# Attention plan with new numbers, and a GpSimd operation per head that waits for VectorE's low part of v

## The chip, the core and the metric

One core of a Trainium2 chip runs the whole program. The metric is the device time of one execution in microseconds (us), taken as the median of several runs. Engines go by the profile's names: PE is TensorE (PEld its weight loads), DVE is VectorE, ACT is ScalarE, POOL is GpSimd, SP is SyncE, which issues the DMAs.

## The reference, cut to what matters

```python
def _attn_ref(q, k, v):                       # 2 x 8 heads, 1152 x 64
    q_pool = q.reshape(B, H, S // 2, 2, D).mean(axis=3)      # 576 queries
    scores = scale * np.matmul(q_pool, k.transpose(0, 1, 3, 2))
    scores = scores - np.max(scores, axis=-1, keepdims=True)
    attn = np.exp(scores)
    attn = attn / (np.sum(attn, axis=-1, keepdims=True) + 1e-09)
    return np.matmul(attn, v)
def reference(...):
    x = attention, heads side by side         # 1152 x 512
    x = _moe_ref(x, ...)                      # 4 experts: relu(x @ w1) @ w2, weighted
    return _moe2_ref(x, ...)                  # ((x@w1) * (x@w2)) @ w3 @ w_out
```

All of it is wanted in fp32 accuracy, so operands are split in a high and a low 16-bit part and multiplied in several passes.

## The kernel before

Attention goes by pairs of heads: pair i (0 to 7) holds heads s = 0 and s = 1; the first four pairs belong to batch 0, the others to batch 1. The work of a head is planned with these names, which are also the tiles' names in the rows:

- `plan_k`, `plan_q` (for the next pair): PE transposes k (kt, in two groups) and the pooled q (qt); ACT copies the high parts (kab, qh, and QZ, a bf16 copy of q); DVE subtracts to the low parts (kl line 281, ql line 332). A small cast of QZ stands on POOL (line 336), and POOL also pools q (QP, lines 246 and 249).
- `plan_max` (for the next pair): for nine blocks of queries PE makes rough scores mp (three matmuls of 384 columns, line 399) and DVE reduces them to maxima mx (two reductions, line 402); end of a head: mf (lines 416 to 419), a transpose mr on PE, a cast mh on ACT, and two small DMAs (lines 439, 440) that put the maxima into row 0 of Q2.
- `plan_v`: DVE takes v's row maxima (vm, line 468), PE spreads them (vp, line 472), and three short DVE operations (lines 456 to 460) make the scale vs. `v_hi` is the high part of v on ACT (line 521). `v_lo` is its low part on DVE: one SCALAR_TENSOR_TENSOR of 128 x 576 elements, line 525, two inputs in SBUF, one per head.
- `plan_scores`: per head nine chunks c: PE makes s (four matmuls, line 546), ACT takes the exponential pf (line 556), POOL subtracts the high half to get the low part pl (TENSOR_TENSOR 128 x 576, line 567, both inputs in SBUF). With two PSUM buffers for s, chunk c + 2 waits for pf of chunk c.
- `plan_av`: 135 small matmuls av per head (lines 589, 591), spread over the time of the next head; the first 27 need all nine chunks of pf and pl. `out_of` (DVE, lines 595 to 606) divides and stores; for batch 1 it has one operation more (XT, line 606).

PE's scratch tiles in PSUM are `work(0)` and `work(1)`, with one buffer each: kt, qt, mp, mr and vp take turns in them, and each waits until the one before has been read.

Nothing orders this at run time but the queues. Every step is put on an agenda with a time in chunks (`at(t, f)`), a head being 9 and a pair 18 of them; the agenda is sorted by that time and the steps are recorded in that order, so each engine's queue is the agenda's order. The numbers at the head of the file (lines 11 to 84) are those times. Semaphores for data and buffers are added by the framework. After the agenda, the experts and the last layers are recorded in a fixed order.

```python
def v_lo(i, s):
    src = rv[i][:, s, :].rearrange("p (c d) -> p c d", d=D)
    nc.vector.scalar_tensor_tensor(
        out=vt[s][:, :, 0:64], in0=src, scalar=vs[i][:, s : s + 1], in1=vt[s][:, :, 64:128],
...
nc.gpsimd.tensor_tensor(out=o, in0=f, in1=h, op=ALU.subtract)      # pl
```

Of the kernel before, what the change touches and what calls it, by code (L numbers as in the profile page):

```python
# [9 lines left out]

TURN = 0.985
TURNS = (1.141, 1.53, 3.03)
TURN0 = (0.042, 0.45, 0.848)
KH = 0.39
KL_ = 0.22
QH_ = 1.05
QL_ = 0.218
M0 = 0.122
M1 = 0.01
M2 = 0.49  # L20
LO_DVE = ((), ())
LASTD = ((3,), (1, 6))
LOL = 2.043
EX = 0.728
EX2 = 0.85
LO = 3.649
LOV = 1.281
AV0 = 1.49
AVN = 7.43
AVW = ((1.06, 0.102, 0.51, 0.636, 1.56, 0.106, 0.4, 2.814), (0.861, 0.24, 1.106, 3.116, 1.062, 0.51, 0.69, 1.54))  # L30
VH = 0.57
VL = 1.96
VL0 = -1.66
VR = 4.22
VE = 0.962
V1 = (5.587, 1.434)
VL1 = 7.087
QZ0 = 0.149
QZ1 = 0.0
VLZ = 2.729  # L40
K0 = 1.197
Q0 = 0.51
L0 = (5.7, 5.655)
LV2 = 16.124
PQ = 1.38
PQS = -2.45
SH = -6.018
XR = 138.482
CX = 129.207
CXT = (0, 0.419, 0.7, 1.3, 1.3)  # L50
LK1 = -10
LQ1 = -10
LV1 = -9
V0 = -8
V0E = -5.866
WARM = 39
WARM_K = 10
WARM_N = 5
WARM_E = 45
WARM_T = 8  # L60
VH0 = 1.5
FIRST = (0.71, 1.14, 2.08, 3.212)
NEAR = 0.0
LATER = 0
KT = (3.05, 4.25)
QT = 4.94
MX0 = (7.048, 8.195, 9.5, 11.42, 13.11)
SPOS = ((0, 1.3, 1.8, 2.8, 4.254, 4.9, 5.614, 6.855, 8.026), (-0.075, 0.604, 1.815, 2.935, 4.1, 4.548, 5.55, 6.8, 7.711))
AVS = 0.02
AVP = 1.7  # L70
MXF = (7.173, 8.254, 9.678, 11.809, 13.01)
MX1 = (14.249, 16.073, 17.228, 18.72)
ME = 0.17
SW = 130.75
W1 = 133.8
WT = ((124.735, 129.6, 130.611, 132.455, 138.5, 133.3, 133.5, 135.131, 135.8), (4.4, 8.95))
WN = (1, 4, 5, 3, 0)
WN2 = (1, 4, 4, 3, 0)
WS = 6
XA = 0.2  # L80
XS = 0.35
XC = (0.88, 1.1)
UA = 135.2
US = 2.59
DT = (140.727, 144.042)
OUT = 0.65
XB = 147.376
DS = 1.912
TICKS = ((), (), (), (0, 1), (), (2,), (0, 4, 13), (2, 9), (), (0, 2, 10), (2, 8, 9), (14,), (0, 10), (2,), (2, 6, 14), (2, 4, 7), (0, 1))
FT = ((7,), (5,), (3,), (4,), (7,), (3,), (), (4,))  # L90
GT = ((0, 2), (2,), (0, 1, 2), (0, 2), (0, 1), (0, 1), (), (0,))
# [13 lines left out]
ALU = mybir.AluOpType  # L105
# [12 lines left out]
def tile_kernel(ctx: ExitStack, tc: tile.TileContext, q, k, v, dp, w1, w2, mw1, mw2, mw3, mwo, out):  # L118
    nc = tc.nc
# [78 lines left out]
    QP = k_p.tile([P, NB + 1, 2, D], F32, name="QP")  # L198
# [39 lines left out]
    def at(t, f, *args):  # L238
        agenda.append((t, len(agenda), f, args))


    def pool_q(i, n):
        eng = nc.gpsimd if i else nc.vector
        if n < 2:
            x = rq[i][:, n]
            eng.tensor_tensor(out=QP[:, :NB, n, :], in0=x[:, :, 0, :], in1=x[:, :, 1, :], op=ALU.add)
        else:
            x = rt[i]
            eng.tensor_tensor(out=QP[:TL, NB], in0=x[:, :, 0, :], in1=x[:, :, 1, :], op=ALU.add)

    def work(g, name):

# [5 lines left out]
    def plan_k(i, t):  # L258
# [7 lines left out]
        for g in range(2):  # L266
# [54 lines left out]
    def plan_q(i, t, tv):  # L321
# [55 lines left out]
    def plan_max(i, s, times):  # L377
# [141 lines left out]
    def v_hi(i, s):  # L519
        src = rv[i][:, s, :].rearrange("p (c d) -> p c d", d=D)  # L520
        nc.scalar.activation(out=vt[s][:, :, 64:128], in_=src, func=AF.Copy, scale=vs[i][:, s : s + 1])

    def v_lo(i, s):
        src = rv[i][:, s, :].rearrange("p (c d) -> p c d", d=D)
        nc.vector.scalar_tensor_tensor(  # L525
            out=vt[s][:, :, 0:64], in0=src, scalar=vs[i][:, s : s + 1], in1=vt[s][:, :, 64:128],
            op0=ALU.mult, op1=ALU.subtract,
        )
# [3 lines left out]
    def plan_scores(i, s, t):  # L532
        for c in range(NC):
            st = {}

            def pe(c=c, st=st):
                if c == 0:
                    if i + s:
                        pft[i, s] = ph_p.tile([P, NC, T], F32, tag="pf", name=f"pf{i}_{s}")
                    pht[i, s] = pft[i, s].bitcast(BF16).rearrange("p c (t w) -> p c t w", w=2)[:, :, :, 1]  # L540
                    plt[i, s] = ph_p.tile([P, NC, T], F16, tag="pl", name=f"pl{i}_{s}")
                ps = st["s"] = ps_s.tile([P, 2, 512], F32, tag="s", name=f"s{i}_{s}_{c}")
                cs = slice(c * P, (c + 1) * P)
                for a, b, first in ((K2, Q2, True), (K1, Q1, False)):
                    for n in range(2):
                        mm(  # L546
                            ps[:, n, :HALF], a[s][:, cs], b[s][:, n * HALF : (n + 1) * HALF],
                            start=first, stop=not first,
                        )

            two = lambda ap: ap.rearrange("p (n t) -> p n t", n=2)

            on_dve = c in (LO_DVE[s] if i < NPAIR - 1 else LASTD[s])

            def whole(c=c, st=st):
                nc.scalar.activation(out=two(pft[i, s][:, c, :]), in_=st["s"][:, :, :HALF], func=AF.Exp, scale=SCORE)  # L556

            def again(c=c, st=st):
                x = st["s"][:, :, :HALF]
                nc.scalar.activation(out=x, in_=x, func=AF.Exp, scale=SCORE)  # L560

            def lo(c=c, st=st, on_dve=on_dve):
                o, f, h = plt[i, s][:, c, :], pft[i, s][:, c, :], pht[i, s][:, c, :]
                if on_dve:
                    nc.vector.tensor_tensor(out=two(o), in0=st["s"][:, :, :HALF], in1=two(h), op=ALU.subtract)
                else:
                    nc.gpsimd.tensor_tensor(out=o, in0=f, in1=h, op=ALU.subtract)  # L567

            u = t + (SPOS[s][c] if i else c)
            at(u, pe)  # L570
            at(u + EX, whole)
            if on_dve:
                at(u + EX2, again)
            at(u + (LOV if on_dve else LO if i < NPAIR - 1 else LOL), lo)

    def plan_av(i, s, t, span):
# [287 lines left out]
    with tc.manual_schedule():  # L864
# [489 lines left out]
```

## Time and profile before

| what | us |
|---|---|
| median of 3 runs (801.87 to 801.97) | 801.97 |
| the profiled execution | 798.73 |
| its span, first to last instruction | 796.9 |
| PE busy in the span | 777.3 |
| DVE busy | 592.3 |
| ACT busy | 398.9 |
| POOL busy | 293.9 |

The clock granted to PE was full in the whole span. Attention runs from about 18 us to about 238 us of the span; the experts and the last layers follow. In a row of the trace the first number is the start in us from the start of the span; a matmul's duration contains its pipeline's latency, so the pace of PE is read from start to start. A number in brackets is the engine's idle time just before, and what ended it.

### The profile page before, as it was taken

Reading aid. Unit: us, or ns where it says so; the run is one execution under the profiler, and the core shown is the slowest. Engines: PE = TensorE matmul, PEld = TensorE weight load, DVE = VectorE, ACT = ScalarE, POOL = GpSimd, SP = SyncE. Lnnn points to the kernel's source line nnn. Section 1 sums busy time; section 2 is a strip of 40 time slices with the busy share of each in tenths; the row PEclk is TensorE's granted clock in tenths of the full one; section 3 lists DMA queues with packets and bytes.
Section 4 is the critical chain, followed back from the end, with each engine's and each line's share of the span. In section 5 each row is a group of like instructions: output and inputs, shape, how many; then the busy total and the mean of one; then the engine's idle time right before and its main releaser. Section 6 shows DMA issues by size and latency. Waiting matters only on the chain.

```text
span 796.9 us, 15559 instructions
## 1 busy us (share of the span) xinstructions
PE 777.3 (98%) x6301; PEld 493.3 (62%) x6301; DVE 592.3 (74%) x1048; ACT 398.9 (50%) x722; POOL 293.9 (37%) x277
## 2 busy tenths in 40 slices
PE   8799999999999999999999999999999999999998
PEld 6588778877775555555555455554544445655787
DVE  6989898888956577789789999979978866872000
ACT  3666666656746432355334667544545544553111
POOL 5888988898640000011001223203331314343100
PEclk9999999999999999999999999999999999999999
DMA  7876676665311311223223242212367832200111
GB/s 176 211 169 146 167 176 146 154 148 125 91 29 53 106 53 54 80 82 116 93 68 93 79 131 79 83 53 79 107 132 151 176 109 80 80 1 1 27 40 53
DMA packets 86656, 79.68 MB, mean 100 GB/s; under 512 B 50425, under 2 KB 69113, under 8 KB 86585
## 3 DMA queue, kind: packets, MB, share of 16 engines
q1 hardware_dynamic: 86584, 78.70, 38.3%
q8 instruction: 49, 0.80, 0.4%
q14 instruction: 23, 0.18, 0.1%
HBM read 51.92 MB, written 2.36 MB: 68 GB/s over the span
## 4 chain that ended last, share of the span: by engine, by line
PE 75%; DVE 19%; DMA 3%; ACT 1%; issue 1%; SPq 0%; ACTq 0%
PE dn L760 19%; PE up L720 18%; PE gt L1292 12%; PE o L1308 6%; DVE mx L402 6%; PE wf L1261 5%; PE s L546 4%; PE mp L399 3%; PE av L591 3%; DVE vt L525 3%; DMA rw<-in_moe_w 2%; PE av L589 1%; DVE kl L281 1%; DVE vm L468 1%; DVE w L691 1%
## 5 line engine op out<-in xcount | busy, mean ns | idle before, releaser
L760 PE MATMUL dn<-w,h 128*128 128x512 f16 x840 | 184.1, 379 | 0.4 <-DVE h L731 0.4
L567 POOL TENSOR_TENSOR pl<-pf 128x576 f16<-128x576 f32 x141 | 164.4, 1196 | 10.9 <-ACT pf L556 10.3
L720 PEld LDWEIGHTS <-w 128*128 128x128 f16 x1152 | 111.6, 98 | 76.3 <-DVE w L691 1.0
L760 PEld LDWEIGHTS <-h 128*128 128x128 f16 x840 | 81.4, 98 | 96.7 <-issue 1.0
L556 ACT ACTIVATE pf<-s 128x576 f32<-128x576 f32 x144 | 93.0, 650 | 48.6 <-PE s L546 47.4
L402 DVE TENSOR_REDUCE mx<-mp 128x1 f32<-128x768 f32 (+1 forms) x144 | 101.9, 751 | 19.2 <-PE mp L399 16.7
L720 PE MATMUL up<-xB,w 128*128 128x320 f16 x768 | 109.9, 299 | 0.5 <-DVE xB L809 0.5
L859 POOL TENSOR_TENSOR wo<-wo,cv_a 128x512 f32<-128x512 f32 x20 | 25.8, 1292 | 225.0 <-DVE wo L856 126.9
L726 ACT ACTIVATE up<-up 128x320 f32<-128x320 f32 (+1 forms) x96 | 45.9, 478 | 115.3 <-PE up L720 103.6
L546 PE MATMUL s<-Q,K 128*128 128x288 bf16 (+1 forms) x576 | 96.4, 313 | 1.1 <-ACT pf L556 0.9
L720 PE MATMUL up<-xA,w 128*128 128x512 f16 x384 | 89.1, 379 | 0.3 <-DVE w L691 0.3
L591 PE MATMUL av<-vt,pl 128*128 128x65 f16 x720 | 84.9, 195 | 0.0
L591 PE MATMUL av<-vt,pf 128*128 128x65 f16 x720 | 83.7, 193 | 1.2 <-DVE XT L606 1.1
L589 PE MATMUL av<-vt,pf 128*128 128x64 f16 x720 | 83.0, 193 | 0.0
L731 DVE TENSOR_TENSOR h<-up,h 128x320 f16<-128x320 f32 (+1 forms) x94 | 50.2, 551 | 43.7 <-ACT h L727 43.3
L1292 PEld LDWEIGHTS <-mw 128*128 128x128 f16 x576 | 55.9, 98 | 37.0 <-issue 0.3
L591 PEld LDWEIGHTS <-pf 128*128 128x128 bf16 x720 | 67.1, 99 | 14.9 <-issue 5.6
L591 PEld LDWEIGHTS <-pl 128*128 128x128 f16 x720 | 66.9, 97 | 5.3 <-issue 1.3
L589 PEld LDWEIGHTS <-pf 128*128 128x128 bf16 x720 | 67.2, 97 | 4.6
L399 PE MATMUL mp<-kab,QZ 128*128 128x384 bf16 x216 | 51.8, 333 | 4.9 <-DVE mx L402 3.8
L774 DVE SCALAR_TENSOR_TENSOR x2B<-dn,sh,x2B 128x512 f32<-128x512 f32 x75 | 52.9, 744 | 4.7 <-PE dn L760 4.0
L1292 PE MATMUL gt<-x2Bt,mw 128*128 128x320 f16 x384 | 53.5, 299 | 0.0
(182 smaller groups left out, 1165.5 us busy)
## 6 DMA issues: line engine op xcount, KB each, us to landing
rw<-in_moe_w SPq DMA_DIRECT2D x64, 512.0 KB
K<-kab SPq DMA_DIRECT2D x32, 288.0 KB
rk<-in_k SPq DMA_DIRECT2D x16, 288.0 KB
rv<-in_v SPq DMA_DIRECT2D x8, 576.0 KB
rq<-in_q SPq DMA_DIRECT2D x8, 512.0 KB
rw<-in_moe_w_out SPq DMA_DIRECT2D x8, 512.0 KB
Q<-qh SPq DMA_DIRECT2D x16, 144.0 KB
Q<-ql SPq DMA_DIRECT2D x16, 144.0 KB
```

What stands on the lines that cost most here:

```text
L399: mm(ps[:, n, :PC], QZ[:, o : o + P], upper(KAB[i])[:, sl], start=True, stop=True)
L402: nc.vector.tensor_reduce(out=mx[i, s][:, j, g : g + 1], in_=st.pop((j, g))[:, :, :PC], axis=AX.XY, op=ALU.max)
L546: mm(ps[:, n, :HALF], a[s][:, cs], b[s][:, n * HALF : (n + 1) * HALF], start=first, stop=not first,)
L556: nc.scalar.activation(out=two(pft[i, s][:, c, :]), in_=st["s"][:, :, :HALF], func=AF.Exp, scale=SCORE)
L567: nc.gpsimd.tensor_tensor(out=o, in0=f, in1=h, op=ALU.subtract)
L589: mm(t[:, j, 0:D], p, vt[s][:, c, 0:D], start=False, stop=False)
L591: mm(t[:, j, :], p, vt[s][:, c, D:], start=(c == 0 and n == 0), stop=(c == NC - 1 and n == 2))
L720: mm(p, w[:, a, c, fc * P : (fc + 1) * P], x[b][:, c, lo - o : hi - o], start=(c == 0 and a == b), stop=(c == KD - 1 and a == 1),)
L731: nc.vector.tensor_tensor(out=hl[:, fc, lo:hi], in0=st["p"], in1=hh[:, fc, lo:hi], op=ALU.subtract)
L760: mm(p, hid[n][a][:, fc, t * P : (t + 1) * P], w[:, b, fc, :], start=(fc == 0 and a == b), stop=(fc == 1 and a == 1),)
L774: nc.vector.scalar_tensor_tensor(out=acc, in0=st["p"], scalar=share, in1=acc, op0=ALU.mult, op1=ALU.add)
L1292: mm(p, mws[n][:, a, m * KD + c], x[:, b * KD + c, lo - o : hi - o], start=(c == 0 and a == b), stop=(c == KD - 1 and a == 1),)
```

## The change

Two things are changed. First, all but a few of the numbers of the attention's plan have new values, so that the order on every engine between the first scores and the last attention output is another. (The order after that, on all engines, and the count and kind of all instructions but the waits are the same.) The two that the prediction's mechanism speaks of:

```diff
-LO = 3.649
+LO = 2.818
-QZ1 = 0.0
+QZ1 = 2.96
```

`LO` is the time from a chunk's scores to its pl on POOL; `QZ1` moves the cast of QZ on POOL.

Second, a dependency is added: from some time after `v_lo` on the agenda (`hold`, at an offset `GD`), the next POOL operation of `pool_q` or pl waits on a semaphore until that `v_lo` has finished.

```diff
+GD = ((0.148, 0.12), (0.148, -4.656), (0.047, 0.629))
...
+    behind = []
+
+    def port_wait(ins):
+        while behind:
+            tc.add_manual_dep(
+                ins.ins, behind.pop().ins.name,
+                mybir.DependencyInfo(mybir.DependencyClass.Sync, mybir.DependencyReason.DATA), reason="port",
+            )
...
+        if i:
+            port_wait(ins)
...
+    def hold(i, s):
+        behind.append(vl[i, s])
...
-        nc.vector.scalar_tensor_tensor(
+        vl[i, s] = nc.vector.scalar_tensor_tensor(
...
-                    nc.gpsimd.tensor_tensor(out=o, in0=f, in1=h, op=ALU.subtract)
+                    port_wait(nc.gpsimd.tensor_tensor(out=o, in0=f, in1=h, op=ALU.subtract))
...
+                at(
+                    t + 9 * s + (VL if i + s else VL1) + (VLZ if i == NPAIR - 1 and not s else 0)
+                    + max(0.001, GD[0 if i == 0 else 2 if i == NPAIR - 1 else 1][s]), hold, i, s,
+                )
```

On POOL, from the last QP of pair 2's second head to the first QP of pair 3's (`pl_0` and `pl_1` are a pair's two heads; `x3` counts equal rows that follow each other), this stands before:

```order
L246 TENSOR_TENSOR QP<-rq_1585 128x4x64
L567 TENSOR_TENSOR pl_1_1684<-pf_1_1683 128x576 [waits Activation_49]
L567 TENSOR_TENSOR pl_0_1953<-pf_0_1952 128x576 [waits Activation_49] x3
L336 CAST QZ<-qh_2106 64x64 [waits DMAHW0_49,Activation_49,Pool_49]
L567 TENSOR_TENSOR pl_0_1953<-pf_0_1952 128x576 [waits Pool_49]
L567 TENSOR_TENSOR pl_0_1953<-pf_0_1952 128x576 x2
L567 TENSOR_TENSOR pl_0_1953<-pf_0_1952 128x576 [waits Activation_49] x3
L567 TENSOR_TENSOR pl_1_2242<-pf_1_2241 128x576 [waits Activation_49] x3
L249 TENSOR_TENSOR QP<-rq_2143 64x128 [waits DMAHW4_49]
```

and this in the changed kernel, where lines are about 10 to 17 further on:

```order
L256 TENSOR_TENSOR QP<-rq_1556 128x4x64
L584 TENSOR_TENSOR pl_1_1692<-pf_1_1691 128x576 [waits Activation_49]
L584 TENSOR_TENSOR pl_0_1961<-pf_0_1960 128x576 [waits DVE_49,Activation_49]
L584 TENSOR_TENSOR pl_0_1961<-pf_0_1960 128x576 [waits Activation_49] x6
L348 CAST QZ<-qh_2095 64x64 [waits DMAHW0_49,Pool_49]
L584 TENSOR_TENSOR pl_0_1961<-pf_0_1960 128x576 [waits Activation_49,Pool_49]
L584 TENSOR_TENSOR pl_0_1961<-pf_0_1960 128x576 [waits Activation_49]
L584 TENSOR_TENSOR pl_1_2250<-pf_1_2249 128x576 [waits DVE_49,Activation_49]
L584 TENSOR_TENSOR pl_1_2250<-pf_1_2249 128x576 [waits Activation_49] x5
L259 TENSOR_TENSOR QP<-rq_2114 64x128 [waits DMAHW2_49]
```

The first pl of each head now waits for DVE (that is `v_lo` of the same head; so in 13 of the 16 heads, in the other three it is a later pl), the cast of QZ stands behind seven pl of head 0 instead of three, and the first QP behind six pl of head 1 instead of three.

On DVE, from `v_lo` of pair 3, head 0, on, before:

```order
L525 SCALAR_TENSOR_TENSOR vt_119<-rv_1314,vs_1575,vt_119 128x9x64
L281 TENSOR_TENSOR kl_2024<-kt_0_2025,kab_2023 128x768
L468 TENSOR_REDUCE vm<-rv_1872 128x2
L281 TENSOR_TENSOR kl_2024<-kt_1_2056,kab_2023 128x384
L456 TENSOR_SCALAR vp_2129<-vp_2129 128x2
L459 TENSOR_SCALAR vs_2133<-vp_2129 128x2
L460 RECIPROCAL vs_2133<-vs_2133 128x2
L332 TENSOR_TENSOR ql_2107<-qt_2108,qh_2106 128x576
L402 TENSOR_REDUCE mx_0_2184<-mp_0_0_0_2185 128x1
```

and in the changed kernel:

```order
L542 SCALAR_TENSOR_TENSOR vt_119<-rv_1326,vs_1588,vt_119 128x9x64
L293 TENSOR_TENSOR kl_2033<-kt_0_2034,kab_2032 128x768
L480 TENSOR_REDUCE vm<-rv_1884 128x2
L293 TENSOR_TENSOR kl_2033<-kt_1_2067,kab_2032 128x384
L344 TENSOR_TENSOR ql_2096<-qt_2097,qh_2095 128x576
L468 TENSOR_SCALAR vp_2144<-vp_2144 128x2
L471 TENSOR_SCALAR vs_2146<-vp_2144 128x2
L472 RECIPROCAL vs_2146<-vs_2146 128x2
L414 TENSOR_REDUCE mx_0_2159<-mp_0_0_0_2160 128x1
```

`v_lo` keeps its place; ql goes ahead of the three short operations on vp. On PE, vp itself moves back past chunk 6 of the scores: it stood 13 av behind qt and 8 av ahead of chunk 6, and stands now 8 av behind chunk 6 and one av ahead of chunk 7.

## Rows read from the trace of the kernel before

**Rows 1.** Busy time in pair 2 (instruction counts in brackets): PE, PEld, DVE, ACT, POOL.
```profile
72.30:98.00 25.70, 25.09 (x394) 20.67 (x391) 22.51 (x37) 16.37 (x27) 22.52 (x23) 1.00 0.68 158
```

**Rows 2.** Timeline of PE: the first scores of pairs 1, 2 and 7, and work between.
```profile
46.68 0.29 PE L546 MATMUL s<-Q,K 128*128 128x288 bf16 x1
...
71.16 0.19 PE L591 MATMUL av<-vt,pf 128*128 128x65 f16 x1
...
72.36 0.67 PE L546 MATMUL s<-Q,K 128*128 128x288 bf16 x4
72.86 0.68 PE L399 MATMUL mp<-kab,QZ 128*128 128x384 bf16 x3
73.39 0.28 PE L546 MATMUL s<-Q,K 128*128 128x288 bf16 x1
...
75.55 0.82 PE L275 MATMUL kt<-ident,rk 128*128 128x128 f32 x6
76.20 0.19 PE L589 MATMUL av<-vt,pf 128*128 128x64 f16 x1
...
201.88 0.29 PE L546 MATMUL s<-Q,K 128*128 128x288 bf16 x1
```

**Rows 3.** Waits of PE from 46.6 to 201.8: waiting, releaser, us, times, longest.
```profile
PE vp L472 <- DVE kl L281: 2.8, 5, 0.6
PE mp L399 <- DVE mx L402: 1.5, 2, 1.0
```

**Rows 4.** Timeline of DVE in pair 2: `v_lo` of head 0 and of head 1.
```profile
75.03 3.18 DVE L525 SCALAR_TENSOR_TENSOR vt<-rv,vs,vt 128x576 f16<-128x576 f32 x1
...
88.30 1.11 DVE L525 SCALAR_TENSOR_TENSOR vt<-rv,vs,vt 128x576 f16<-128x576 f32 x1
```

**Rows 5.** Timeline of POOL at the same two places.
```profile
74.25 1.14 POOL L567 TENSOR_TENSOR pl<-pf 128x576 f16<-128x576 f32 x1
...
76.46 1.14 POOL L567 TENSOR_TENSOR pl<-pf 128x576 f16<-128x576 f32 x1
80.70 0.24 POOL L336 CAST QZ<-qh 64x64 bf16<-64x64 f32 x1 [3.10 <-ACT qh L341]
...
87.65 1.15 POOL L567 TENSOR_TENSOR pl<-pf 128x576 f16<-128x576 f32 x1
88.75 1.66 POOL L567 TENSOR_TENSOR pl<-pf 128x576 f16<-128x576 f32 x1
```

**Rows 6.** Groups by form, six pairs, 46.6 to 201.8: busy, mean ns, idle before.
```profile
L525 DVE SCALAR_TENSOR_TENSOR vt<-rv,vs,vt 128x576 f16<-128x576 f32 x12 | 24.6, 2047 | 0.1
L336 POOL CAST QZ<-qh 64x64 bf16<-64x64 f32 x6 | 1.4, 236 | 18.5 <-ACT qh L341 18.5
```

**Rows 7.** Timelines of ACT and PE behind `v_lo` of pair 2, head 0.
```profile
76.40 0.80 ACT L278 CAST kab<-kt 128x768 fp32r<-128x768 f32 x1 [0.40 <-PE kt L275]
...
80.11 0.20 PE L591 MATMUL av<-vt,pl 128*128 128x65 f16 x1
80.86 0.16 PE L472 MATMUL vp<-vm,ones 128*128 128x2 bf16 x1 [0.56 <-DVE kl L281]
```

**Rows 8.** Group of `v_lo` in the start, 18.4 to 46.6.
```profile
L525 DVE SCALAR_TENSOR_TENSOR vt<-rv,vs,vt 128x576 f16<-128x576 f32 x2 | 3.0, 1504 | 0.0
```

**Rows 9.** Waits of PE from 201.8 to 238.
```profile
PE cxs L505 <- DVE cxd L499: 1.0, 1, 1.0
PE av L591 <- DVE XT L606: 0.7, 1, 0.7
PE s L546 <- ACT pf L556: 0.4, 1, 0.4
```

**Rows 10.** Timelines at the end of pair 2: the maxima's way into Q2.
```profile
93.96 0.28 PE L431 MATMUL mr<-ident,mf 128*5 128x128 f32 x1
...
95.27 0.57 SPq L440 DMA_DIRECT2D Q<-mh  x1
...
98.00 0.29 PE L546 MATMUL s<-Q,K 128*128 128x288 bf16 x1
```

More of the change, by code (lines that the diff above doesn't have):

```diff
@@ L9 @@
 from concourse.masks import make_identity
[L11 to L20, printed above, removed]
+TURN = 3.555
+GD = ((0.148, 0.12), (0.148, -4.656), (0.047, 0.629))
+TURNS = (1.142, 1.493, 3.629)
+TURN0 = (0.083, 0.258, 0.54)
+KH = 0.382
+KL_ = 0.464
+QH_ = 0.909
+QL_ = 0.255
+M0 = 0.294
+M1 = 0.053
+M2 = 0.544
 LO_DVE = ((), ())
 LASTD = ((3,), (1, 6))
-LOL = 2.043
-EX = 0.728
-EX2 = 0.85
-LO = 3.649
[L27 to L38, printed above, removed]
-QZ1 = 0.0
[L40 to L50, printed above, removed]
+LOL = 1.108
+EX = 0.875
+EX2 = 1.273
+LO = 2.818
+LOV = 1.349
+AV0 = 1.465
+AVN = 7.434
+AVW = ((1.006, 0.189, 0.456, 1.103, 2.218, -0.152, 0.496, 2.371), (1.38, 0.222, 0.981, 1.353, 0.516, 0.465, 0.623, 3.149))
+VH = 0.186
+VL = 1.955
+VL0 = -1.6
+VR = 4.684
+VE = 2.062
+V1 = (5.572, 1.3)
+VL1 = 4.402
+QZ0 = 1.767
+QZ1 = 2.96
+VLZ = 3.247
+K0 = 1.182
+Q0 = 0.729
+L0 = (6.916, 7.28)
+LV2 = 16.819
+PQ = 1.98
+PQS = -1.222
+SH = -6.577
+XR = 138.621
+CX = 129.332
+CXT = (-1.517, 0.272, 0.807, 1.275, 1.369)
 LK1 = -10
@@ L53 @@
 LV1 = -9
-V0 = -8
-V0E = -5.866
+V0 = -11.66
+V0E = -3.294
 WARM = 39
@@ L61 @@
 VH0 = 1.5
-FIRST = (0.71, 1.14, 2.08, 3.212)
+FIRST = (0.766, 1.197, 2.625, 3.192)
 NEAR = 0.0
 LATER = 0
[L65 to L68, printed above, removed]
+KT = (3.029, 4.153)
+QT = 4.899
+MX0 = (7.123, 8.247, 9.544, 11.574, 13.11)
+SPOS = ((0.006, 0.826, 1.96, 2.838, 4.094, 4.818, 5.84, 6.917, 7.782), (0.109, 0.604, 2.254, 3.229, 2.589, 4.276, 5.633, 6.663, 7.87))
 AVS = 0.02
-AVP = 1.7
-MXF = (7.173, 8.254, 9.678, 11.809, 13.01)
-MX1 = (14.249, 16.073, 17.228, 18.72)
+AVP = 3.594
+MXF = (7.305, 8.292, 10.033, 11.751, 13.167)
+MX1 = (14.225, 16.042, 17.275, 18.704)
 ME = 0.17
-SW = 130.75
-W1 = 133.8
-WT = ((124.735, 129.6, 130.611, 132.455, 138.5, 133.3, 133.5, 135.131, 135.8), (4.4, 8.95))
+SW = 130.647
+W1 = 133.717
+WT = ((124.588, 128.907, 130.95, 132.388, 139.583, 133.448, 134.51, 135.298, 136.522), (7.306, 10.818))
 WN = (1, 4, 5, 3, 0)
@@ L80 @@
 XA = 0.2
[L81 to L88, printed above, removed]
+XS = 0.378
+XC = (0.859, 1.144)
+UA = 135.352
+US = 2.657
+DT = (141.08, 144.604)
+OUT = 0.488
+XB = 150.338
+DS = 0.379
 TICKS = ((), (), (), (0, 1), (), (2,), (0, 4, 13), (2, 9), (), (0, 2, 10), (2, 8, 9), (14,), (0, 10), (2,), (2, 6, 14), (2, 4, 7), (0, 1))
@@ L245, in pool_q @@
             x = rq[i][:, n]
-            eng.tensor_tensor(out=QP[:, :NB, n, :], in0=x[:, :, 0, :], in1=x[:, :, 1, :], op=ALU.add)
+            ins = eng.tensor_tensor(out=QP[:, :NB, n, :], in0=x[:, :, 0, :], in1=x[:, :, 1, :], op=ALU.add)
         else:
             x = rt[i]
-            eng.tensor_tensor(out=QP[:TL, NB], in0=x[:, :, 0, :], in1=x[:, :, 1, :], op=ALU.add)
+            ins = eng.tensor_tensor(out=QP[:TL, NB], in0=x[:, :, 0, :], in1=x[:, :, 1, :], op=ALU.add)
+        if i:
+            port_wait(ins)
     def work(g, name):
@@ L521, in v_hi @@
         nc.scalar.activation(out=vt[s][:, :, 64:128], in_=src, func=AF.Copy, scale=vs[i][:, s : s + 1])
+    vl = {}
+    def hold(i, s):
+        behind.append(vl[i, s])
     def v_lo(i, s):
         src = rv[i][:, s, :].rearrange("p (c d) -> p c d", d=D)
-        nc.vector.scalar_tensor_tensor(
+        vl[i, s] = nc.vector.scalar_tensor_tensor(
             out=vt[s][:, :, 0:64], in0=src, scalar=vs[i][:, s : s + 1], in1=vt[s][:, :, 64:128],
```

## The prediction

> **What bounds the kernel now.** Read first the busy shares. Over the whole span PE is busy 777.3 of 796.9 us, and everything behind attention keeps its order, so the question is only what PE loses between the first scores and about 238 us. The stretch of pair 2 [rows 1] shows three full engines: PE 25.09, DVE 22.51 and POOL 22.52 of 25.70 us. PE's figure flatters it, because a matmul's duration holds its latency. So the second view is PE's timeline, read from start to start [rows 2]. Six pairs, from pair 1's first scores at 46.68 to pair 7's at 201.88, take 155.2 us, 25.87 each. What they would take without a wait: a score chunk takes 72.86 - 72.36 = 0.50, a block mp 73.39 - 72.86 = 0.53, and one av (72.36 - 71.16) / 39 = 0.031, 39 of them standing between those two rows; six kt take 76.20 - 75.55 = 0.65, 0.11 each. A pair has 18 chunks, 9 blocks, 270 av and 9 kt; five qt, two mr and one vp are estimated at kt's pace as 0.8 together. That is 9.0 + 4.8 + 8.3 + 1.0 + 0.8 = 23.9 us. So up to 2.0 us of each pair is waiting, or switching between kinds of work, and 11.8 us over the six.
>
> **Who makes PE wait.** The waits of PE [rows 3] name DVE: vp waits for kl in five pairs (0.6 each) and mp for mx. In pair 2 the av before vp starts at 80.11 and vp at 80.86 [rows 7], a loss of 0.72 beside the pace of 0.03. DVE in turn loses its time in one operation, `v_lo`. In pair 2 it takes 3.18 us for head 0 and 1.11 for head 1, for the same 128 x 576 elements [rows 4]; its mean over twelve is 2.05 [rows 6].
>
> POOL's rows tell why [rows 5]. At head 0, three pl run back to back, from 74.25 to 76.46 + 1.14 = 77.60, and `v_lo` ends at 78.21: 0.61 us after the last of them. At head 1, pl ends at 87.65 + 1.15 = 88.80 and `v_lo` at 89.41: again 0.61 later. But here it is the next pl that is stretched, to 1.66 instead of 1.14. So `v_lo` needs 0.61 us alone, doesn't run while a pl runs, and POOL's next operation either keeps it out or is kept out itself. At head 0 it lost to three in a row.
>
> The Trainium skill has a rule on this, and it speaks against the change ("SBUF — State Buffer", section "Who interferes with whom"): a VectorE instruction with two SBUF inputs shares a port pair with GpSimd's reads, and whoever issues first holds it for that one instruction. By that rule `v_lo` would have been let in at 75.39, when the pl that was running ended, and would have taken 0.97 us; a wait on POOL could then save it nothing. The trace agrees on the exclusion and not on the turn: 3.18 us are measured.
>
> **The change, part by part.**
>
> *The wait.* In 13 of the 16 heads the first pl of a head waits for that head's `v_lo`, so POOL has nothing to put in its way but the operation that runs already. `v_lo` then takes 0.61 if POOL is idle and 0.61 + 1.14 = 1.75 at worst. I take 0.9, nearer the lower end: the new order has POOL earlier (below), so mostly it will stand and wait. On DVE that frees 3.18 - 0.9 = 2.3 us at head 0 and 0.2 at head 1, 2.5 per pair. It doesn't all reach the path. Behind `v_lo` of head 0 stands kl, which needs kab, ready at 76.40 + 0.80 = 77.20 [rows 7]; kl now starts at 78.14, so 0.9 us move forward there. That covers the 0.72 that vp loses. At head 1 it moves the following mx by 0.2 to 0.5, which is what mp waits for [rows 3].
>
> *What the wait costs POOL.* Queued behind the waiting pl are all other pl, and PE's 27th av of the next head needs the ninth. POOL's own work in a pair is 22.52 less the 0.52 of stretching: 22.0 us. Against a pair of 24.6 that leaves 2.6 us to stand still, 1.3 per `v_lo`. A wait costs 0.61 at least, about 0.7 with its signal, and more where POOL comes early. Coming early is cheap, since it is time that POOL had in hand. The move of QZ's cast pays for it: POOL stands 3.10 us before that cast [rows 5], 18.5 over six pairs [rows 6], with pl behind it that were ready; now seven pl instead of three go first, while ACT makes qh.
>
> *The moved steps.* vp on PE goes back past a score chunk (0.50 more room) and stands behind ql on DVE, which reads the qt tile that mp needs next: both loosen the same waits. The three short DVE operations that then come behind ql delay vs, which is first read a head later. The rest of the table spreads chunks, blocks and av anew; its work is the same, and I cost its moves at nothing, with the 0.7 below as a margin. What is late next, with `v_lo` out of the way: kab on ACT for kl, and the third mp of a block, which waits for the second mx of the block before.
>
> *The three stretches.*
> - Six pairs: I take 24.6 each, the pace of 23.9 and 0.7 left for switching and small waits: 155.2 - 6 x 24.6 = 7.6 us. Ends: nothing, and all of it, 11.8.
> - The start (18.4 to 46.6): two `v_lo` take 3.0 us [rows 8] on a DVE that is full there; alone they would take 1.2. Saving between 0 and 1.8; I take 0.7, since POOL still runs without a gap when the first comes up.
> - The end (201.8 to 238): PE waits 2.1 us in three places [rows 9]. Six matmuls of dn instead of three (512 columns each; an estimate by mp's pace, 0.53 us for three of 384, gives 0.24 apiece) now stand between the last av of head 0 and the first of head 1, over the 0.7 for XT; 28 more av stand ahead of the scores that waited 0.4; cxs keeps its chain. Between 0 and 2.1; I take 0.6.
>
> Sum: 7.6 + 0.7 + 0.6 = 8.9 us. From the profiled execution's 798.73 that gives 789.8. The median of the runs shown, 801.97, lies 3.24 above that execution, so the time to be measured is **793.1 us**. All upper ends together are 15.7 us, or 786.3; the lower end is no gain, 802.0.
>
> **The rivals.**
>
> *The order gives half back.* A plan with many numbers changed can tighten one thing while it loosens another. One such place: the maxima must land in Q2 before the next pair's first scores. Now PE has 98.00 - 93.96 = 4.04 us of work between mr and those scores, of which the second small DMA is issued after 95.27 + 0.57 - 93.96 = 1.88 [rows 10]; 2.16 are left for landing, and that is enough, as no such wait is listed. In the new order ten av fewer stand there, 0.3 us less. If landing needs all of the 2.16, that is 0.3 x 7 = 2 us lost; with a second place like it, 4 to 5 of the 8.9 go: 797.0 to 800.4 us.
>
> *The wait does nothing.* If DVE's freed time is only idle time (kl waiting for kab, mx waiting for mp) and the waits come back in other places, or if POOL would have let `v_lo` in behind a single pl in any case, as at head 1 [rows 5], and the long ones are of no account, the time stays within 800.4 to 803.6. (That is also what the Trainium skill's rule of the turn, cited above, would come to.) Against it: vp's wait stands directly behind the long `v_lo` in five pairs.
>
> *POOL becomes the bound, and the kernel is slower.* The place is the first pl of each head. If POOL comes to it long before DVE reaches `v_lo`, which has the reductions of two blocks and the division of the head before it in its queue, POOL stands still, falls behind, and PE waits for the ninth pl. Slower than now begins where POOL's 22.0 us and two waits exceed 25.87: from 1.9 us per wait. At 2.3 a pair takes 22.0 + 4.6 = 26.6, 0.7 more than now, and six pairs 4.4 more: 806 us. For it: POOL is as full as DVE [rows 1]. Against it: two waits of 1.9 are more than three times what `v_lo` needs.
>
> *All of it goes*, pairs at the bare pace: 786.3 to 789.8.
>
> **How the numbers follow.** Chances: forecast (789.8 to 797.0) 0.56, half given back 0.23, nothing 0.08, POOL the bound 0.07, all of it 0.06. The range must hold 8 in 10: the forecast and the first rival, 789.8 to 800.4. A measurement of this kernel can tell about 0.2%, 1.6 us, from no change. So faster by over 0.2% is 0.56 + 0.23 + 0.06 = 0.85, within it 0.08, slower 0.07.
>
> **What would show it.** In the changed profile `v_lo` should have a mean of about 0.9 over the six pairs and no instance above 1.8; the wait of vp should be gone from PE's list, and mp's nearly; POOL should show waits for `v_lo` of 0.5 to 2 us per head, with less than half of the 18.5 us before QZ; and pairs should be 24.3 to 24.9 us apart. I am wrong on the mechanism if `v_lo` still takes over 2 us in any of the six pairs, wrong on the path if it is short and pairs still take over 25.3, and the last rival but one is right if PE waits for pl.

## The result, and the profile after

The changed kernel took 787.69 us (median of 5, 786.75 to 790.44) against 801.89 us before (median of 5); the ratio is 0.9834, with a 95% interval of 0.9809 to 0.9858. On another chip, later, it took 787.22 against 799.97, a ratio of 0.9845 (0.9832 to 0.9858). The sign was forecast; the gain was larger than forecast (793.1 us, with a range from 789.8), and the time fell outside the range.

The trace after is of an execution of 787.69 us with a span of 785.9. First, the busy time of pair 2 (columns as in [rows 1], which it answers to):

```profile
70.59:94.73 24.14, 24.14 (x392) 20.34 (x389) 19.86 (x37) 16.17 (x27) 22.04 (x23) 1.00 0.72 167
```

The pair takes 24.14 us instead of about 25.67, and PE is busy in all of them. DVE has 19.86 us of work where it had 22.51, for the same 37 instructions. The waits of PE from 46.5 to 192.4, which answer to [rows 3], have no row left. (Such a list holds an engine's idle times over 0.15 us. In pairs 5 and 6, which take 24.72 and 24.70, PE still loses 0.57 us each, spread over the av behind XT and the mp behind mx.) `v_lo` over the same six pairs (its group: count, then minimum, median and maximum in ns), and what POOL waits for (waiting, releaser, us, times, longest):

```profile
L542 DVE SCALAR_TENSOR_TENSOR vt<-rv,vs,vt x12: 808/814/1028, 49.4 to 183.0; 128x576 f16<-128x576 f32 x12
```

```profile
POOL pl L584 <- DVE vt L542: 5.9, 5, 1.6
POOL pl L584 <- ACT pf L573: 4.6, 4, 1.2
POOL pl L584 <- ACT mh L447: 2.3, 3, 0.8
```

All twelve `v_lo` are short, where before the mean was 2.05 us [rows 6]. POOL stands for `v_lo` and no longer before QZ. How the wait works at head 0 of pair 2 is seen in the timelines of DVE and of POOL, which answer to [rows 4, 5]:

```profile
73.57 0.84 DVE L542 SCALAR_TENSOR_TENSOR vt<-rv,vs,vt 128x576 f16<-128x576 f32 x1
```

```profile
72.65 1.14 POOL L584 TENSOR_TENSOR pl<-pf 128x576 f16<-128x576 f32 x1
74.56 2.25 POOL L584 TENSOR_TENSOR pl<-pf 128x576 f16<-128x576 f32 x2 [0.76 <-ACT mh L447]
```

A pl ends at 72.65 + 1.14 = 73.79; the next, the first of the head, starts at 74.56, 0.15 after `v_lo` ends at 74.41. The profile puts POOL's 0.76 down to mh on ACT; the order of the kernel says that this pl waits for `v_lo`, and the times fit it. All twelve waits of the list end 0.14 to 0.15 us after a `v_lo`, so the rows with mh and with pf belong to `v_lo` as well: 12.8 us in all, 0.76 to 1.6 per head.

Where the 11.0 us between the two traced executions (798.73 and 787.69) went, by stretches:

| stretch | before | after | saved |
|---|---|---|---|
| to the first scores of pair 0 | 18.43 | 18.53 | -0.10 |
| pair 0 | 28.25 | 27.93 | 0.32 |
| pairs 1 to 6 | 155.20 | 145.98 | 9.22 |
| pair 7, to the last av | 35.07 | 34.25 | 0.82 |
| behind the last av (same order) | 559.97 | 559.21 | 0.76 |

The last row holds the part whose order the change leaves alone; in the experiments below it lies between 559.0 and 560.3, so 0.76 is scatter.

### The profile page after: what moved, and what is told of

It is laid out like the page before. It is cut to its first block, busy times and chain, and to the rows that moved or that the text cites. A ratio compares the mean times of both kernels' runs of the same rounds, so it can differ in the third digit from the quotient of the medians.

```text
span 785.9 us, 15567 instructions
## 1 busy us (share of the span) xinstructions
PE 772.2 (98%) x6301; PEld 491.6 (63%) x6301; DVE 578.4 (74%) x1048; ACT 397.4 (51%) x722; POOL 288.8 (37%) x277
## 4 chain that ended last, share of the span: by engine, by line
PE 92%; DVE 5%; DMA 1%; ACT 1%; issue 1%; SPq 0%; ACTq 0%
PE dn L777 23%; PE up L737 22%; PE gt L1313 12%; PE s L563 8%; PE o L1329 6%; PE av L608 6%; PE wf L1282 5%; PE mp L411 4%; PE av L606 3%; DVE mx L414 2%; PE kt L287 1%; DMA rk<-in_k 1%; DMA rw<-in_moe_w 1%; PE qt L341 0%; DVE vt L542 0%
## 5 line engine op out<-in xcount | busy, mean ns | idle before, releaser
L584 POOL TENSOR_TENSOR pl<-pf 128x576 f16<-128x576 f32 x141 | 159.3, 1159 | 24.9 <-ACT pf L573 12.5
L573 ACT ACTIVATE pf<-s 128x576 f32<-128x576 f32 x144 | 91.1, 647 | 41.4 <-PE s L563 41.0
L411 PE MATMUL mp<-kab,QZ 128*128 128x384 bf16 x216 | 50.2, 333 | 2.0 <-DVE mx L414 1.5
```

The source lines that it names most:

```text
L411: mm(ps[:, n, :PC], QZ[:, o : o + P], upper(KAB[i])[:, sl], start=True, stop=True)
L584: port_wait(nc.gpsimd.tensor_tensor(out=o, in0=f, in1=h, op=ALU.subtract))
```

## The experiments

Two theories stood at the start. A: the wait makes `v_lo` short, the short `v_lo` frees DVE, and that is the gain. B: the new order alone gives the gain, with the wait as an insurance. All ratios are to the kernel before on the same chip, with their 95% intervals; "six pairs" are pairs 1 to 6, from first scores to first scores.

### The changed plan without the wait

```diff
 def hold(i, s):
-    behind.append(vl[i, s])
+    pass
```

> The changed plan, with no GpSimd operation waiting for v_lo (the order on every engine is that of the changed kernel). Theory A (the wait makes v_lo short, and the short v_lo makes the pairs short): v_lo is kept out by back-to-back pl again, its mean over pairs 1 to 6 is 1.8 to 2.8 us instead of 0.83, pairs take 24.8 to 25.5 us instead of 24.1 to 24.7, and the time is 792 to 797 us. Theory B (the new order does it, the wait is only an insurance): v_lo may be long or not, but pairs stay at 24.1 to 24.7 and the time within 1.6 us of 787.7. Theory C (the order without the wait is worse than the order before): above 800 us.

Measured: 796.33 us (0.9951, 0.9939 to 0.9963). The time is theory A's, but the places are not. The six pairs take 148.14 us, 7.06 less than before, although nothing waits for `v_lo`; a pair is 24.42, 0.28 above the changed kernel, although `v_lo` of head 0 takes 2.81 in pairs 2 to 4. What the wait is worth lies in pair 0, 33.98 us instead of 27.93. DVE, POOL and PE's wait there:

```profile
25.97 7.40 DVE L542 SCALAR_TENSOR_TENSOR vt<-rv,vs,vt 128x576 f16<-128x576 f32 x1
33.30 0.94 DVE L293 TENSOR_TENSOR kl<-kt,kab 128x768 bf16<-128x768 f32 x1
```

```profile
26.10 6.66 POOL L584 TENSOR_TENSOR pl<-pf 128x576 f16<-128x576 f32 x6
```

```profile
PE qt L341 <- DVE kl L293: 6.5, 1, 6.5
```

POOL had six pl ready in a row, and `v_lo` came in after the sixth: 26.10 + 6.66 = 32.76, and 0.61 later, at 33.37, it ends. Behind it stood kl, behind kl PE's qt. PE did nothing for over 6 us, and the clock that it was granted fell with it (columns as in [rows 1]; the last but two is the granted clock):

```profile
30.00:34.00 4.00, 0.00 (x0) 0.00 (x0) 4.00 (x2) 0.00 (x0) 2.76 (x3) 0.61 0.99 209
34.00:38.00 4.00, 3.61 (x17) 2.89 (x18) 3.12 (x7) 2.16 (x4) 0.48 (x2) 0.53 0.27 93
```

0.53 is close to the lower level, 1.2 of 2.4 GHz, while PE was working again. Of the 6.05 us, 4.5 are the longer wait for kl (6.5 against 2.0); the other 1.5 are put down to the clock, by difference. By stretches the wait is worth 6.05 in pair 0, 2.16 in the six pairs and 0.54 at the end: 8.75, where the spans of the two traces differ by 794.6 - 785.9 = 8.7.

### The wait in pair 0 alone

```diff
 def hold(i, s):
-    behind.append(vl[i, s])
+    if i == 0:
+        behind.append(vl[i, s])
```

> The changed kernel with the wait in pair 0 alone; in the seven other pairs no GpSimd operation waits for v_lo. Without any wait the trace lost 6.0 us in pair 0 (where v_lo took 7.4 us and PE's granted clock fell to 0.53) and 2.2 us in the six pairs after it. If the wait is worth most in pair 0, this run has pair 0 at 28 us, the six pairs at 148.1 in all, and a time of 789.5 to 791. If the wait's worth were spread over all pairs (the forecast), this run would be near the run without any wait, 794 to 796.

Measured: 797.69 us (0.9967, 0.9955 to 0.9980). My expectation missed. Pair 0 is good, 28.22, and pairs 2 to 4 take 24.43 as expected; but pair 1 takes 31.78. The same thing happened one pair later:

```profile
49.78 7.67 DVE L543 SCALAR_TENSOR_TENSOR vt<-rv,vs,vt 128x576 f16<-128x576 f32 x1
```

```profile
54.00:58.00 4.00, 0.00 (x0) 0.00 (x0) 4.00 (x2) 0.02 (x1) 2.83 (x3) 0.88 0.79 168
58.00:62.00 4.00, 3.63 (x34) 3.25 (x34) 2.95 (x5) 1.96 (x3) 0.00 (x0) 0.50 0.01 2
```

So it isn't pair 0 that is special. Once POOL has a stock of ready pl, the first `v_lo` without protection is kept out until the stock is used up; after that POOL is no longer behind, and the later `v_lo` take 0.8 to 2.8. In the new order the wait is therefore worth little in each steady pair (0.28) and 6 to 7.4 us once.

### The wait alone, on the first and on the second pl

```diff
-                    nc.gpsimd.tensor_tensor(out=o, in0=f, in1=h, op=ALU.subtract)
+                    port_wait(nc.gpsimd.tensor_tensor(out=o, in0=f, in1=h, op=ALU.subtract))
...
                 at(t + 9 * s + (VL if i + s else VL1) + (VLZ if i == NPAIR - 1 and not s else 0), v_lo, i, s)
+                at(t + 9 * s + (VL if i + s else VL1) + (VLZ if i == NPAIR - 1 and not s else 0) + 1.0, hold, i, s)
```

`port_wait` and `hold` are those of the change; the second run has 2.2 in the place of 1.0.

> The plan of before with the wait alone: the first pl of each head waits for that head's v_lo, as in the changed kernel. Theory A: v_lo falls from a mean of 2.05 to 0.8 to 0.9 us over pairs 1 to 6, vp's wait for kl (2.8 us in all) goes, pairs take 24.6 to 25.2 us instead of 25.9, and the time falls by 4 to 8 us to 794 to 798 us. Theory B (the order does it): v_lo is short, but the waits of PE move to other places (mp for mx, av for x) and the time is within 1.6 us of 801.9. Theory C (POOL falls behind by standing still): PE waits for pl, time above 803.5 us.

> As the run before it, but the second pl of each head waits instead of the first, so that POOL stands still for a shorter time: by the trace of before the first pl of head 0 starts 0.8 us before v_lo is reached, so v_lo should take 0.97 us there (the rest of that pl and 0.61). Theory A: v_lo has a mean of 0.9 to 1.1 over pairs 1 to 6 and the time is within 1.5 us of the run with the wait on the first pl. If POOL's standing still is what costs (theory C), this one is the faster of the two by over 2 us. Theory B: both as before, 801.9.

Measured: 792.60 us (0.9906, 0.9893 to 0.9919) and 797.16 us (0.9964, 0.9952 to 0.9976). With the wait on the first pl `v_lo` has a mean of 0.91, vp's wait is gone from PE's list, pairs 1 to 4 take 24.73 and the six 149.42, 5.78 less than before: theory A's numbers. Set side by side with a pair of before, start to start, the 0.94 us are where the prediction had looked for them: vp behind av 0.72, mp behind the scores 0.21. Theory C falls, POOL's 10.4 us of standing cost PE nothing:

```profile
PE av L607 <- DVE XT L622: 0.5, 2, 0.2
```

```profile
POOL pl L583 <- DVE vt L541: 10.4, 11, 1.7
POOL QZ L347 <- ACT qh L352: 6.2, 6, 1.3
```

On the second pl the same wait gives 4.6 us less, against my expectation of 1.5 at most. DVE and POOL at head 1 of pair 2, and PE's waits from 46.5 to 200.4:

```profile
87.37 1.78 DVE L541 SCALAR_TENSOR_TENSOR vt<-rv,vs,vt 128x576 f16<-128x576 f32 x1
```

```profile
84.07 4.47 POOL L583 TENSOR_TENSOR pl<-pf 128x576 f16<-128x576 f32 x4
```

```profile
PE mp L410 <- DVE mx L413: 3.8, 6, 0.7
```

`v_lo` is reached at 87.37, and the first pl, which is now free, is the last of the four that end at 88.54: `v_lo` lasts 1.78, and mp waits 0.7 for the reduction behind it, once per pair. One pl too late, and DVE's loss shrinks at head 0 (3.18 to 1.26) but grows at head 1 (1.11 to 1.78).

So neither theory is the whole. In the six pairs the wait alone saves 5.78 us, the order alone 7.06 (of which it loses 5.7 again in pair 0), and both together 9.22: they take away in large part the same waits.

### What the rest of the table gives: PE's numbers, then vp, then QZ

Between the wait alone (24.73 a pair) and the changed kernel (24.14) lie 0.59 us. With every interval between two matmuls of a pair set side by side, nearly all of it is mp behind mp (0.28), mp behind av (0.12) and av behind the scores (0.16). The first step added PE's numbers to the wait:

```diff
-M0 = 0.122
+M0 = 0.294
-M1 = 0.01
+M1 = 0.053
-M2 = 0.49
+M2 = 0.544
-AV0 = 1.49
+AV0 = 1.465
-AVN = 7.43
+AVN = 7.434
-AVW = ((1.06, 0.102, 0.51, 0.636, 1.56, 0.106, 0.4, 2.814), (0.861, 0.24, 1.106, 3.116, 1.062, 0.51, 0.69, 1.54))
+AVW = ((1.006, 0.189, 0.456, 1.103, 2.218, -0.152, 0.496, 2.371), (1.38, 0.222, 0.981, 1.353, 0.516, 0.465, 0.623, 3.149))
-MX0 = (7.048, 8.195, 9.5, 11.42, 13.11)
+MX0 = (7.123, 8.247, 9.544, 11.574, 13.11)
-SPOS = ((0, 1.3, 1.8, 2.8, 4.254, 4.9, 5.614, 6.855, 8.026), (-0.075, 0.604, 1.815, 2.935, 4.1, 4.548, 5.55, 6.8, 7.711))
+SPOS = ((0.006, 0.826, 1.96, 2.838, 4.094, 4.818, 5.84, 6.917, 7.782), (0.109, 0.604, 2.254, 3.229, 2.589, 4.276, 5.633, 6.663, 7.87))
-AVP = 1.7
+AVP = 3.594
-MX1 = (14.249, 16.073, 17.228, 18.72)
+MX1 = (14.225, 16.042, 17.275, 18.704)
```

> The kernel before with the wait on the first pl and with those numbers of the changed plan that set when PE's chunks, blocks and av come and when DVE reduces (SPOS, AVW, AV0, AVN, AVP, MX0, MX1, M0, M1, M2); the numbers for k, q, QZ, v and GpSimd stay those of before. The wait alone left pairs at 24.73 us, 0.59 above the changed kernel: 0.4 in mp waiting for mx, 0.16 in av behind the scores. If it is the interleaving of chunks, blocks and av that takes these away (the forecast cost these moves at nothing), pairs 1 to 4 take 24.1 to 24.3 us and the time is 789 to 791 us. If it is the rest of the table (ql ahead of the operations on vp, kl, QZ), pairs stay at 24.6 to 24.8 and the time at 792.0 to 793.5.

Measured: 792.96 us (0.9919, 0.9904 to 0.9934); pairs 2 to 4 at 24.79. No gain, but other waits. Those three are gone, and vp waits again:

```profile
PE vp L483 <- DVE kl L292: 3.0, 6, 0.5
```

Next, vp was moved too, together with QZ0 (for pair 0, below):

```diff
-VR = 4.22
-VE = 0.962
+VR = 4.684
+VE = 2.062
...
-QZ0 = 0.149
+QZ0 = 1.767
```

> The run before with the wait and PE's numbers, and three numbers more from the changed plan: VR and VE, which put vp behind chunk 6 of the scores and behind ql on VectorE, and QZ0, the place of QZ's cast in pair 0. Without them pairs 1 to 4 took 24.79 us, and set side by side with a pair of the changed kernel all of the 0.65 between them was vp waiting for kl (PE's av to vp 682 ns instead of 35); pair 0 took 30.06 us because PE waited 2.8 us for an exponential behind QZ's cast. If the gain of the pairs needs these pieces together (short v_lo, the interleave on PE, vp's place) and nothing else of the table, pairs 1 to 4 take 24.1 to 24.3 us, pair 0 27 to 28.5, and the time is 786.5 to 789.5. If moving vp only brings the waits of mp for mx back (as the two stood against each other in the runs before), pairs stay at 24.5 to 24.8 and the time above 790.

Measured: 791.33 us (0.9897, 0.9880 to 0.9913). Pair 0 takes 27.40, as expected; pairs 1 to 4 take 24.63, which neither side had foreseen. vp's wait is gone, and the next one stands in its place, not the one that I named. Interval by interval, a pair now differs from the changed kernel's only here (0.49):

```profile
PE mp L410 <- ACT QZ L353: 1.9, 6, 0.3
```

ACT makes QZ in two casts. Here both stand in front of two exponentials, and the one that mp needs is the second:

```profile
102.42 0.64 ACT L352 CAST qh<-qt 128x576 fp32r<-128x576 f32 x1
103.09 0.62 ACT L349 CAST QZ<-qh 64x512 bf16<-64x512 f32 x1
103.73 0.67 ACT L353 CAST QZ<-qh 64x576 bf16<-64x576 f32 x1
```

In the changed kernel, at the same place, the other cast (line 350) comes only behind the next exponentials:

```profile
101.96 0.64 ACT L353 CAST qh<-qt 128x576 fp32r<-128x576 f32 x1
102.63 0.67 ACT L354 CAST QZ<-qh 64x576 bf16<-64x576 f32 x1
103.22 1.17 ACT L573 ACTIVATE pf<-s 128x576 f32<-128x576 f32 x2
...
105.66 0.62 ACT L350 CAST QZ<-qh 64x512 bf16<-64x512 f32 x1
```

That is `QZ1`: it moves not only the small cast of QZ on POOL, as was said with the change, but also this large one on ACT. The move undone in the changed kernel gives the same wait from the other side:

```diff
-        tz = tv + (QZ0 if i == 1 else QZ1)
+        tz = tv + (QZ0 if i == 1 else QZ1 if i == 0 else 0.0)
```

> The changed kernel with one move undone: from pair 2 on the casts of QZ (the small one on GpSimd, the large one on ACT) stand as early as before, on GpSimd behind four pl of head 0 instead of seven. The wait for v_lo is kept. If GpSimd can only afford the wait because QZ's cast is out of its way (as the forecast had it), GpSimd stands before QZ again by 1 to 3 us per pair, falls behind, and pairs take 24.6 to 25.5 us instead of 24.14: 790 to 796 us. If GpSimd has room for both (22.0 us of work and two waits of 0.75 in 24.14), pairs stay within 0.2 us and the time within 1.6 us of 787.7.

Measured: 790.71 us (0.9882, 0.9868 to 0.9896), pairs 2 to 4 at 24.60. The size is that of the first expectation, the cause is not: POOL doesn't stand before QZ at all, PE stands for ACT:

```profile
PE mp L411 <- ACT QZ L354: 1.7, 6, 0.3
```

The steps together, in us (waits as PE's list has them for pairs 1 to 6; "below the list" are losses that it doesn't show, read from start to start):

| kernel | pairs 2 to 4 | PE waits for | six pairs |
|---|---|---|---|
| before | 25.67 | kl (at vp), mx, XT | 155.20 |
| wait alone | 24.73 | XT; below the list, mx | 149.42 |
| and PE's numbers | 24.79 | kl (at vp) | 149.91 |
| and vp's place | 24.63 | QZ on ACT | 148.95 |
| changed, QZ1 undone | 24.60 | QZ on ACT | 148.82 |
| changed, no wait | 24.42 | mx (pairs 5 and 6); below the list, kl (at qt, 0.26 in all) | 148.14 |
| changed | 24.14 | nothing | 145.98 |

### The kernel before, once more, and with QZ0 alone

The first has no edit; the second is

```diff
-QZ0 = 0.149
+QZ0 = 1.767
```

> The kernel before, once more, with a trace of its own: its five first times were 799.2 and four of 801.87 to 801.97, the execution in the trace took 798.73. If the 3.2 us between them lie in one place (the loads at the start, attention, or the experts' end), an execution of 801.9 in the trace shows that place longer; if the trace shows 798.7 again, nothing can be said. The forecast had put the 3.24 us on top of the sum for the changed kernel too, whose median lies on its own traced execution (787.69).

> The kernel before with one number of the changed plan (QZ0): in pair 0 the large cast of QZ on ACT stands behind two more exponentials, the small one on GpSimd behind one more pl. In the second trace of the kernel before, this cast waited 2.96 us for a small transfer to land, the exponential behind it kept PE waiting for 3.3 us, PE's granted clock fell to 0.68 in the next 4 us, and pair 0 took 30.82 us instead of 28.25. If that is what lifts most runs of before above 799, pair 0 takes 27.5 to 28.5 us here in every run, with no execution above 800 and a median of 798.0 to 799.2. If the offset lies elsewhere: 799.5 to 801.7 as before.

Measured: 800.40 us (1.0007, 0.9997 to 1.0016) and 799.26 us (0.9988, 0.9979 to 0.9997). The second trace of before is of an execution of 802.90, with pair 0 at 30.82 us instead of 28.25. ACT's cast of QZ and PE's wait in pair 0:

```profile
33.90 0.61 ACT L338 CAST QZ<-qh 64x512 bf16<-64x512 f32 x1 [2.96 <-DMA Q<-QZ]
```

```profile
PE s L546 <- ACT pf L556: 3.3, 1, 3.3
```

```profile
30.00:34.00 4.00, 1.40 (x9) 0.81 (x8) 3.62 (x9) 1.01 (x3) 0.91 (x1) 1.00 0.79 191
34.00:38.00 4.00, 2.76 (x12) 1.83 (x12) 1.09 (x2) 3.14 (x5) 3.40 (x4) 0.68 0.97 195
```

The cast may not overwrite QZ before the small transfer of its old contents has landed; ACT stood for that, with exponentials behind it, PE stood for them, and the granted clock fell to 0.68. In the trace that the forecast rests on, the same transfer had come in time. Between the two traces of before, 4.2 us apart, pair 0 holds 2.57, the later first scores (19.21 instead of 18.43) 0.78, pair 1 (26.35 instead of 25.68) 0.67, and the part behind the last av 0.20.

With QZ0 moved, PE's wait for that exponential is not in the list, pair 0 takes 27.29, and the median falls by 0.65 of the 1.25 that separate the median of before from its fastest execution on that chip (799.91 and 798.66). One of eleven executions is above 800 (800.22), and the median of 799.26 is just above the 799.2 that I had set. So this is a part of before's offset, shown; the rest is not. In this run's trace the first scores start at 19.69, and pair 1 takes 26.38 as in the second trace of before: its first `v_lo` takes 3.9 us in both, instead of 3.15, and PE stands for kl once more (this run):

```profile
PE qt L329 <- DVE kl L281: 0.6, 1, 0.6
```

### Two attempts at more

The first `v_lo` of all takes 2.82 us even in the changed kernel, because two pl stand ahead of its wait, and PE waits 2.0 for kl there.

```diff
-VL1 = 4.402
+VL1 = 2.4
```

> The changed kernel with the first v_lo of all (pair 0, head 0) six reductions earlier on VectorE, at a point where GpSimd has no pl to run yet; the first pl waits for it. In the changed kernel this v_lo took 2.82 us, because two pl stood ahead of its wait, and PE then waited 2.0 us for kl. If that wait is v_lo's doing, v_lo takes 0.8 us, PE's wait for kl shrinks by 1 to 2 us, and the time falls by 0.5 to 2 us to 785.7 to 787.2. If kl is held by kab or the maxima that it now delays (0.8 us each), the time is the same or up to 1 us longer.

Measured: 786.86 us (0.9836, 0.9822 to 0.9849); `v_lo` 0.81, pair 0 26.85 instead of 27.93. The 2.0 us of qt are down to 0.4, but a block's mp now waits 0.8 for the reductions behind `v_lo`, and pair 1's first scores lose 0.3 to the transfer of the maxima (24.42). Beside the changed kernel on its own chip (0.9845) the difference can't be told from none: that kernel's trace has the first `v_lo` at 1.73 and pair 0 at 26.84.

> The changed kernel once more, on the chip of the other two runs of this group, as their reference. Its five times were 786.75 to 790.44. In its trace pair 0 had PE waiting 2.0 us for kl at 27.9 us, without the granted clock falling. If its longer executions come from that wait (their mean granted clock was 0.996 to 0.998), times should again spread by 2 to 4 us, while the run with the early v_lo spread by 0.8 (786.57 to 787.40). Pairs 1 to 4 at 24.14.

This, the changed kernel again, is the 787.22 us at the top (787.00 to 788.50): the spread was 1.5, not 2 to 4, and what makes its longer executions isn't settled.

The second attempt puts XT on ACT:

```diff
-                nc.vector.tensor_scalar(
-                    out=XT[r, xd], in0=st["t"][r, NB, :D], scalar1=dn[r, NB:], scalar2=None, op0=ALU.mult
-                )
+                if i < NPAIR - 1:
+                    nc.scalar.activation(out=XT[r, xd], in_=st["t"][r, NB, :D], func=AF.Copy, scale=dn[r, NB:])
```

> The run with the early first v_lo, and XT (64 x 64, the rest of the division in pairs 4 to 6) on ACT instead of VectorE. In the changed kernel pairs 5 and 6 took 24.72 and 24.70 us, 0.57 more than pairs 1 to 4: PE waited 0.23 for XT, and 0.33 for mx behind the second v_lo, which comes 0.29 later. If XT's 0.29 on VectorE is the cause of both, pairs 5 and 6 take 24.14 to 24.3 and the time falls by 0.8 to 1.2 us against the run with the early v_lo alone (786.86), to 785.7 to 786.1. If the exponential behind XT on ACT now makes the scores wait, they stay at 24.6 to 24.8.

Measured: 788.44 us (0.9858, 0.9843 to 0.9872), no gain. Pairs 5 and 6 take 24.91 instead of 24.72. ACT reaches XT early, stands 0.46 us for DVE's division, and the exponentials start behind it:

```profile
143.38 0.31 ACT L624 ACTIVATE XT<-av,dn 64x64 f32<-64x64 f32 x1 [0.46 <-DVE x L618]
143.72 1.19 ACT L573 ACTIVATE pf<-s 128x576 f32<-128x576 f32 x2
```

From start to start a pair now loses 0.29 at the two av that wait for XT and 0.50 at the scores that wait for the exponentials, one place per head; the 0.33 that mp lost is gone. Most of the loss lies behind: pair 7, up to the last av, takes 35.56 us instead of 34.25, and PE stands there for a pl, as in no other place of these runs' pairs 1 to 7:

```profile
PE av L608 <- POOL pl L584: 0.6, 1, 0.6
```

## Why the prediction was right and wrong

**Right.** PE is what the time is read from, and DVE's `v_lo` was a cause of its waits: the wait alone takes the 0.72 at vp away. `v_lo` has the mean of 0.84 that 0.9 was said for; none in the six pairs is above 1.03. POOL had room for the wait: PE waited for no pl, in the change or in the wait alone, so that rival falls. The place of the first rival, the maxima's way into Q2, made no wait either; it shows 0.3 us once, in the run with the early first `v_lo`, and none in two other traces whose pair 0 is as short (26.84 and 26.96). The wait of vp left PE's list, and so did mp's. With the wait alone pairs 1 to 4 took 24.73 each, next to the 24.6 of the sum. Two readings of the rows were off without harm: alone `v_lo` needs 0.81, not 0.61, and at head 0 it lost two turns, not three, since the first of the three pl was running already.

**Wrong, the moved steps.** The step "the rest of the table spreads chunks, blocks and av anew; its work is the same, and I cost its moves at nothing, with the 0.7 below as a margin" failed. The rest of the table took most of the margin away: pairs 1 to 4 stand at 24.14, with no wait in PE's list and 0.24 above the pace of 23.9, and the six pairs saved 9.22 instead of 7.6. What hid it is the chain in the table above: each piece alone uncovers the next wait (PE's numbers give nothing without vp's place, vp's place 0.16 without QZ1's); with the whole table it is 0.59 a pair. That these pieces and nothing else of the table make the 0.59 was read from the intervals; the run with them alone was not made.

**Wrong, what QZ's move is for.** "The move of QZ's cast pays for it" put its worth on POOL. It is on ACT: undone, mp waits for QZ, 0.46 a pair, and POOL has no wait before QZ.

**Wrong, the offset.** This step carried the time out of the range. Of the 5.4 us between forecast and measurement the sum of 8.9 has 2.1, against 11.0 between traces (1.6 in the six pairs, 0.8 scatter behind the last av, -0.3 in the rest); the other 3.24 come from "lies 3.24 above that execution, so the time to be measured is **793.1 us**". That offset belonged to the kernel before. A part of it is ACT's wait for a transfer in pair 0, and QZ0, which I counted among the moves that cost nothing, takes this place away. The changed kernel's median is its traced execution. Had the offset held, the 11.0 would have given 790.9, inside the range. So it is in part luck that the rival "all of it goes", at 0.06, has 787.69 in its 786.3 to 789.8: this too was counted from 801.97 and asks 12.2 to 15.7 us of the change, and in the six pairs its 11.8 is further from 9.22 than the 7.6 is.

**Half right, the wait itself.** Forecast as 2.5 us on DVE in every pair, it came as 2.6 (22.45 to 19.86, from first scores to first scores). But in the new order DVE could have spared most of that: without the wait a steady pair is 0.28 longer. Its worth there is that `v_lo` is never kept out for 7 us, which costs 6 to 7.4 once, the clock included. By the Trainium skill ("SBUF — State Buffer", section "Who interferes with whom") whoever issues first gets the shared port pair for its whole instruction. Read as a turn, as the prediction read it, this would have `v_lo` in after one pl; here six went ahead of it, in each of two runs, so the measurement decides against that reading.

The small terms: the start gave 0.32 (0.7 said), the end 0.82 (0.6 said). Pairs 24.3 to 24.9 us apart were to be the sign; they came in below it.

## What to carry to other kernels

When a schedule of many numbers changes, price the whole chain of next waits, or take the pace without any wait as one end that can well be reached: waits that stand behind one another can give little one by one and much together, as here. Where VectorE must get past a run of ready GpSimd operations, let the very first of them wait for it; one operation later the gain was here 4.6 us smaller. And explain an offset between a traced execution and the median before you add it to another kernel's sum: this one did not carry over.

## What the runs showed of the hardware that I had not expected

- `v_lo` takes 0.81 us with POOL idle, and ends 0.61 after the last pl where it had to wait: the first 0.2 of it pass while it is kept out.
- Whether it gets in between two back-to-back pl isn't a matter of who came first: in [rows 4, 5] it starts before the pl that follows at both heads. In the trace of before it lost twice running in head 0 of pairs 1 to 4, and got in at the first such change in head 1 of the same pairs; in the two runs above it lost six. What decides it stays open.
- Where PE had stood still for 2.8 to 6.5 us (five traces), the granted clock of the next 4 us was 0.50 to 0.68, with PE at work. In the run without the wait that came to 1.5 us on top of the stall, by difference; with the wait in pair 0 alone, in pair 1, to 31.78 - 24.43 - 5.0 = 2.35 (PE's list has 5.0 us for kl there). The length of the stop alone does not tell: in pair 0 of that same run PE stood only 1.5 us for kl, and the stretch behind it shows 0.61, while the 2.0 us of the changed kernel left the clock at 1.00:

```profile
30.00:34.00 4.00, 3.81 (x19) 2.62 (x17) 3.13 (x8) 3.37 (x6) 3.86 (x5) 0.61 0.82 171
```
